# A block-sparse attention with a channel mix: every engine's order planned anew, with other transfer constants

## The chip, the cores and the metric

The kernel runs on one core of a Trainium2 chip. The metric is the device time of one execution in microseconds (us); less is better. The core has five engines with an instruction stream of its own each: PE (matrix products; its weight loads, PEld, run beside them), DVE, ACT and POOL (element-wise work), and SP, which here issues the transfers from and to HBM. An engine works its stream strictly in order, and waits where an instruction needs what another engine or a transfer hasn't finished.

## The reference

Attention over 24 blocks of 32 positions (4 batches, 8 heads, 768 positions, head size 64). A block of queries sees its own block and both neighbours, blocks 0 and 23, and three sampled blocks; the queries of blocks 0 and 23 see everything. A channel mix follows, in which a token is blended with the one before it.

```python
scores = scale * np.matmul(q, k.transpose(0, 1, 3, 2))
mask = np.abs(blk_i - blk_j) <= window
mask = mask | (blk_i == 0) | (blk_j == 0) | (blk_i == n_blocks - 1) | (blk_j == n_blocks - 1)
for qb in range(n_blocks):
    for kb in sampled_blocks[qb]:
        mask[qb * block:(qb + 1) * block, kb * block:(kb + 1) * block] = True
scores = np.where(mask, scores, -1000000000.0)
attn = np.exp(scores - np.max(scores, axis=-1, keepdims=True))
attn = attn / (np.sum(attn, axis=-1, keepdims=True) + 1e-09)
x = np.matmul(attn, v)            # heads joined: (4, 768, 512)
xk = mu_k * x + (1.0 - mu_k) * x_prev
xr = mu_r * x + (1.0 - mu_r) * x_prev
k = np.maximum(xk @ w_k, 0.0)     # (512, 1024)
v = k * k @ w_v                   # (1024, 512)
r = 1.0 / (1.0 + np.exp(-(xr @ w_r)))
return r * v
```

## The kernel before

**Attention** is cut into 26 units. Four wide units (numbers 0 to 3, in the order 0, 1, 3, 2 here) hold the queries of blocks 0 and 23 of one batch each and all 768 keys. Twenty-two near units (4 to 25) hold one block of queries each, for all batches, and eight blocks of keys. A unit goes through these steps, in two halves: PE makes the scores `s` (`sw` in a wide unit; L608, L559); DVE takes their maxima `nm` (L613 to L618, L567); ACT the exponentials `p` (L539); PE transposes them into `t` (L523), ACT copies these into `pt` (L527); PE multiplies by the values `VA` into `o` (L639, L585); DVE divides into `x` (L657 to L661), PE transposes it (L668), ACT puts it into the mixer's tile `xt`. There are two PSUM buffers each for scores, for `o`, and for transposes (the latter shared with the mixer).

**The sampled blocks** are numbers in HBM. Two small transfers bring them and a table of constants (`number` and `con`, L307 and L308), 17 rows on DVE (L316 to L336, "the pack") drop those that the mask holds already and write them into `packed`; SP reads `packed` (L425) and issues the transfers of the sampled keys (L488) and values (L505) of every near unit.

**The mixer** has 12 tiles of 256 tokens. A tile has two gates `r_0p`, `r_1p` (12 matmuls each, L776), four hidden parts `h_0p` to `h_3p` (24 each, L794) whose squares ACT and POOL make in the buffers tagged "kk" (L807 to L811), and two products with w_v (L823). A product is made of three terms in a rounded format, for which each operand is split in a high and a low part.

**The weights** come as 64-bit numbers in 20 chunks (0 to 3 of w_r, 4 to 11 of w_k, 12 to 19 of w_v; 512 KB each) and are converted on the chip: ACT makes `wmag` (L373), also in a "kk" buffer, of which there are three; DVE makes `wf` of it in three steps (L378, L382, L386); POOL splits that (L396, L400). The first twelve are loaded into eight slots (`early_w`), the last eight (`raw`) into buffers that they share with the exponentials `p`.

**The order** is not written out. The code declares operations with their cost, their reads and writes and a rank (a due time), and `Plan.order` goes through a model of the five engines: at each step it takes, for each engine, the operation of lowest rank among those that could start within `NEAR` ns of the first, and emits the one that ends first. A transfer takes its bytes over `RATE` (bytes per ns) in that model, on one queue, and is noticed `DONE` ns later; eight may be under way (`FLIGHT`). Buffers are given out in the same pass. So the constants of the model and the table of due times at the end of the file fix the order of all engines and which operation gets which buffer. The ranks are sums such as these:

```python
plan.add(DVE, 4000, PICK + 3, pack, reads=[(number,), (con,)], writes=[(r,), (e,), (packed,)])
at = RAW_AT[i] if i < 3 * CC else rank
at_k, at_v = at - LEAD_K, at - LEAD_V
plan.add(PE, N_PV, t1 + O_PV[kind], pv, ...)
```

`UNIT_AT` holds the due times of the units, `MIX_AT` of the mixer tiles, `RAW_AT` of the early weight loads, `WEIGHT_AT` of the conversions, `PICK` of the pack and its two transfers, `LEAD_*` how long before a unit its loads are due, `O_*` the distances of a unit's steps.

## Time and profile before

| | us |
|---|---|
| three runs | 571.64, 572.94, 573.92 (median 572.94) |
| the profiled execution | 571.98 |
| its span, from the first to the last instruction | 570.2 |
| PE busy | 537.7 |
| DVE, ACT, POOL busy | 269.6, 325.2, 291.0 |
| mean granted PE clock | 0.987 |

The span is cut off at the first and last instruction; 1.78 us of the execution lie around it. In rows of a timeline the first number is the start, the second the busy time of the row, then engine, line, operation and tiles (buffer numbers left out), and in brackets how long the engine was idle ahead of it and what ended that. Releasers are worked out from semaphore events: where an instruction waits for several, the one named can be one that was long done.

### The profile page before, as it was taken

The numbers are of one execution on the slowest core, as the hardware profiler recorded it, in microseconds if no ns is written. First come the engines' busy times: TensorE is split into PE (matmuls) and PEld (weight loads), VectorE is DVE, ScalarE is ACT, GpSimd is POOL, SyncE is SP. The second block draws the span as 40 slices with busy tenths as digits, with TensorE's granted clock in tenths as the row PEclk, the third lists the DMA queues.
The fourth block names the chain that finished last, engine by engine and source line by source line (L and its number), as shares of the span: only waits on it lengthen the run. The fifth ranks groups of instructions, "written<-read, shape, count | busy, mean of one in ns | idle before, by whom it ended". The sixth has DMA issues, their size and how long they took to land.

```text
span 570.2 us, 18311 instructions
## 1 busy us (share of the span) xinstructions
PE 537.7 (94%) x7724; PEld 438.5 (77%) x7724; DVE 269.6 (47%) x533; ACT 325.2 (57%) x612; POOL 291.0 (51%) x359
## 2 busy tenths in 40 slices
PE   6788778979999999999999999999999999999997
PEld 2454556856887798897798798887877989889886
DVE  0877998887445353434424524433452242142411
ACT  0676687768478468467464756546564356424330
POOL 0430456887266066346066285373383663448752
PEclk9799899999999999999999999999999999999999
DMA  8999899773653553362651804135510302110001
GB/s 314 395 398 342 295 343 352 260 228 94 192 182 95 172 164 116 112 189 76 189 167 29 278 24 157 36 100 166 169 39 20 95 19 84 32 39 1 20 20 38
DMA packets 34183, 86.09 MB, mean 151 GB/s; under 512 B 5010, under 2 KB 5780, under 8 KB 31124
## 3 DMA queue, kind: packets, MB, share of 16 engines
q1 hardware_dynamic: 34100, 84.92, 44.5%
q8 instruction: 61, 1.00, 0.7%
q14 instruction: 22, 0.18, 0.1%
HBM read 78.60 MB, written 6.29 MB: 149 GB/s over the span
## 4 chain that ended last, share of the span: by engine, by line
PE 80%; DVE 9%; DMA 4%; ACT 2%; POOL 2%; issue 2%; SPq 0%; DVEq 0%; ACTq 0%
PE v L823 23%; PE o L585 6%; PE s L559 6%; PE t L523 6%; PE r_0p L776 5%; PE h_1p L794 5%; PE h_3p L794 5%; PE h_0p L794 5%; PE h_2p L794 5%; PE r_1p L776 4%; PE tw L523 2%; PE sw L608 2%; DVE nm L567 2%; PE tx L668 2%; DMA raw<-w_v 1%
## 5 line engine op out<-in xcount | busy, mean ns | idle before, releaser
L823 PE MATMUL v<-wv,k 128*128 128x512 f32 (+1 forms) x600 | 145.0, 391 | 0.0
L823 PEld LDWEIGHTS v<-wv,k 128*128 128x128 f32 x600 | 106.8, 188 | 22.8 <-DVE x L661 0.8
L539 ACT ACTIVATE p<-s,nm 128x256 f32<-128x256 f32 x176 | 104.1, 728 | 18.1 <-DVE nm L569 13.8
L567 DVE TENSOR_REDUCE nm<-s 128x4 f32<-128x1024 f32 x44 | 53.6, 1219 | 16.1 <-PE s L559 16.1
L523 PE MATMUL t<-ident,p 128*128 128x128 f32 x352 | 54.6, 278 | 4.7 <-ACT z L783 2.4
L585 PE MATMUL o<-VA,pt 128*32 128x65 f32 x2816 | 49.9, 222 | 6.7 <-ACT pt L527 4.0
L585 PEld LDWEIGHTS o<-VA,pt 128*32 128x32 f32 x2816 | 42.3, 109 | 16.9 <-issue 9.7
L752 POOL TENSOR_TENSOR xr<-xr_1f,xr 128x256 fp32r<-128x256 f32 x24 | 17.7, 737 | 70.8 <-ACT xr L750 70.8
L523 PEld LDWEIGHTS t<-ident,p 128*128 128x128 f32 x352 | 40.2, 140 | 16.1 <-ACT z L783 2.9
L527 ACT COPY pt<-t 128x512 f32<-128x512 f32 x68 | 40.7, 604 | 18.7 <-PE t L523 15.7
L559 PE MATMUL s<-KA,q 64*32 64x256 f32 x1408 | 46.5, 387 | 1.6 <-DVE wf L386 1.2
L743 DVE SCALAR_TENSOR_TENSOR xr_1f<-xr_1d,mk,xt 128x128 f32<-128x128 f32 x48 | 17.9, 372 | 55.9 <-POOL xr L752 46.3
L831 DVE SCALAR_TENSOR_TENSOR z<-v,z 128x512 f32<-128x512 f32 (+1 forms) x25 | 16.8, 670 | 50.1 <-PE v L823 50.0
L685 ACT COPY xt<-tx 128x512 f32<-128x512 f32 x22 | 13.0, 591 | 42.1 <-PE tx L668 42.0
L794 PE MATMUL h_0p<-xk,wk 128*128 128x256 f32 x288 | 37.0, 282 | 0.0
L776 PE MATMUL r_1p<-wr,xr 128*128 128x512 f32 x144 | 36.4, 400 | 0.6 <-ACT h_3k L807 0.6
L794 PE MATMUL h_3p<-xk,wk 128*128 128x256 f32 x288 | 36.4, 281 | 0.0
L743 DVE SCALAR_TENSOR_TENSOR xr_0f<-xr_0d,mk,xt 128x128 f32<-128x128 f32 x48 | 20.3, 424 | 34.0 <-POOL xk L752 13.9
L776 PE MATMUL r_0p<-wr,xr 128*128 128x512 f32 x144 | 36.4, 400 | 0.0
L794 PE MATMUL h_1p<-xk,wk 128*128 128x256 f32 x288 | 36.3, 281 | 0.0
L794 PE MATMUL h_2p<-xk,wk 128*128 128x256 f32 x288 | 36.3, 280 | 0.0
L794 PEld LDWEIGHTS h_0p<-xk,wk 128*128 128x128 f32 x288 | 35.1, 188 | 0.7
(139 smaller groups left out, 940.1 us busy)
## 6 DMA issues: line engine op xcount, KB each, us to landing
VA<-vt SPq DMA_DIRECT2D x93, 260.0 KB, 3.8
KA<-kt SPq DMA_DIRECT2D x90, 256.0 KB, 3.7
VA<-vw SPq DMA_DIRECT2D x24, 260.0 KB, 6.1
KA<-kq SPq DMA_DIRECT2D x16, 384.0 KB, 6.7
out<-z SPq DMA_DIRECT2D x23, 256.0 KB, 2.2
q<-qt SPq DMA_DIRECT2D x22, 256.0 KB, 4.3
early_w<-w_k SPq DMA_DIRECT2D x8, 512.0 KB, 6.4
raw<-w_v SPq DMA_DIRECT2D x8, 512.0 KB, 5.0
```

The source lines that it names most:

```text
L523: nc.tensor.transpose(tp.ap[:, i, :], p.ap[:, x : x + P], ident.ap)
L527: plan.add(ACT, 200 + 0.75 * P * many, rank + 0.1, lambda: nc.scalar.copy(pt.ap[:, 0:many], tp.ap[:, 0:many]), reads=[(tp,)], writes=[(pt,)])
L539: plan.add(ACT, 262 + 0.83 * width, rank, lambda: nc.scalar.activation(turned(p.ap[:, out]), view(), AF.Exp, bias=nm(), scale=SCALE), read ...
L559: nc.tensor.matmul(s.ap[ROWS[j], row, a * 256 : (a + 1) * 256].rearrange("p (n x) -> p n x", x=BLK), q.ap[half, (hp * QB + j) * BLK : (hp ...
L567: nc.vector.tensor_reduce(out=nm.ap.rearrange("p (r a) -> p r a", r=2), in_=s.ap.rearrange("p r (a x) -> p r a x", a=2), axis=AX.X, op=ALU ...
L585: nc.tensor.matmul(o[gi].ap[ROWS[j], i * DV : (i + 1) * DV], pts[row].ap[:, 2 * a + g, ROWS[j]], VA.ap[:, c0 + g, j, h * DV : (h + 1) * DV ...
L743: nc.vector.scalar_tensor_tensor(out=parts(f.ap[:, i, :]), in0=parts(d.ap), scalar=mk.ap[:, which, c : c + 1], in1=cols(c, 1), op0=ALU.mul ...
L752: plan.add(POOL, 80 + 2.4 * MIX * tw, rank + O_MIX, lambda f=f, cs=cs: nc.gpsimd.tensor_tensor(out=dst.ap[:, 1, cs], in0=f.ap, in1=dst.ap[ ...
L776: nc.tensor.matmul(pr.ap[:, 0:512], xr.ap[:, a, c, :], wr.ap[:, w, c, :], start=(c == 0 and m == 0), stop=(c == CC - 1 and m == 2))
L794: nc.tensor.matmul(ph.ap[:, ff * TT : (ff + 1) * TT], wk.ap[:, w, c, f * P : (f + 1) * P], xk.ap[:, a, c, :], start=(c == 0 and m == 0), s ...
L823: nc.tensor.matmul(pv.ap[:, 0:width], k2.ap[:, a, f, i * P : (i + 1) * P], wv.ap[:, w, f, cs], start=(f == 0 and m == 0), stop=(f == FC - ...
L831: plan.add(DVE, 150 + 1.05 * width, done, lambda pv=pv, cs=cs: nc.vector.scalar_tensor_tensor(out=z.ap[:, cs], in0=pv.ap[:, 0:width], scal ...
```

## The change

Two constants of the model of transfers, the due time of the pack, and the table of due times and distances are replaced. No operation is added, removed or altered, and the code of the planner stays as it is; the order that it gives is another on every engine. In the diff, of the table, two lines are shown:

```diff
-    RING, RING_POOL, RATE, DONE, DONE_POOL = 650, 1000, 370, 670, 2600
+    RING, RING_POOL, RATE, DONE, DONE_POOL = 650, 1000, 335, 900, 2600
...
-PICK = -10.949
+PICK = 5.0
...
-LEAD_W, LEAD_Q, LEAD_K, LEAD_V = 31.394, 58.736, 95.899, 26.261
+LEAD_W, LEAD_Q, LEAD_K, LEAD_V = 30.562, 60.235, 742.902, 12.723
-NEAR, STAY, STORE = 34.076, -1.502, 639.005
+NEAR, STAY, STORE = 55.741, 2.392, 639.005
...
```

**The loads of the pack.** On SP, in the wide units' loads, before (four weight loads, the loads of unit 0 and the query of unit 1 stand ahead of these rows; names carry the number of their buffer):

```order
L364 DMA early_w_98<-w_r 128x1024
L471 DMA VA_68<-vw 128x520 x6
L467 DMA KA_67<-kq 128x768 x4
L471 DMA VA_68<-vw 128x520 x4
L461 DMA q3_187<-qt 128x256
L471 DMA VA_68<-vw 128x520 x2
L307 DMA number_262<-blocks 1x144
L308 DMA con_272<-seen 1x462
L364 DMA early_w_98<-w_k 128x1024 x2
L467 DMA KA_67<-kq 128x768 x4
```

and of the change (five weight loads, the loads of unit 0 and the query of unit 1 stand ahead):

```order
L364 DMA early_w_98<-w_k 128x1024
L471 DMA VA_68<-vw 128x520 x6
L364 DMA early_w_98<-w_k 128x1024
L467 DMA KA_67<-kq 128x768 x4
L364 DMA early_w_98<-w_k 128x1024 x2
L461 DMA q3_197<-qt 128x256
L471 DMA VA_68<-vw 128x520 x6
L307 DMA number_375<-blocks 1x144
L308 DMA con_386<-seen 1x462
L467 DMA KA_67<-kq 128x768 x2
```

Before, five weight loads (L364) precede `number` and `con`, and four keys' loads of unit 3 stand behind two further ones. Now nine weight loads precede them, and unit 3's first keys come straight after.

On DVE, where the pack begins, before (`nmw3_0` are maxima of unit 3, the second half that is worked):

```order
L617 TENSOR_TENSOR nmw2_1_616<-nmw2_1_616 128x2
L618 TENSOR_SCALAR nmw2_1_616<-nmw2_1_616 128x2
L613 TENSOR_REDUCE nmw3_0_672<-sw3_0_0_656 128x2
L613 TENSOR_REDUCE nmw3_0_672<-sw3_0_1_674 128x2
L617 TENSOR_TENSOR nmw3_0_672<-nmw3_0_672 128x2
L618 TENSOR_SCALAR nmw3_0_672<-nmw3_0_672 128x2
L316 CAST pickf_691<-number_262 1x72
L318 TENSOR_TENSOR equal_692<-pickf_691,con_272 1x22x7 x2
L320 TENSOR_TENSOR equal_692<-pickf_691 1x22
```

and of the change (`wf8` and `wmag9` are conversions of weight chunks 8 and 9, `nmw1_0` maxima of unit 1):

```order
L613 TENSOR_REDUCE nmw1_0_394<-sw1_0_1_400 128x2
L382 SCALAR_TENSOR_TENSOR wmag8_392<-early_w_98,wmag8_392 128x512
L617 TENSOR_TENSOR nmw1_0_394<-nmw1_0_394 128x2
L618 TENSOR_SCALAR nmw1_0_394<-nmw1_0_394 128x2
L386 SCALAR_TENSOR_TENSOR wf8_440<-early_w_98,wmag8_392 128x512
L378 TENSOR_SCALAR wmag9_405<-wmag9_405 128x512
L316 CAST pickf_475<-number_375 1x72
L318 TENSOR_TENSOR equal_476<-pickf_475,con_386 1x22x7 x2
L320 TENSOR_TENSOR equal_476<-pickf_475 1x22
```

Where it ends now (`nmw3_1` is the first half of unit 3 that is worked):

```order
L334 CAST pickf_475<-pickf_475 1x48
L335 TENSOR_SCALAR packed_69<-pickf_475 1x24
L336 TENSOR_TENSOR packed_69<-packed_69,pickf_475 1x24
L613 TENSOR_REDUCE nmw3_1_548<-sw3_1_0_510 128x2
L613 TENSOR_REDUCE nmw3_1_548<-sw3_1_1_543 128x2
L382 SCALAR_TENSOR_TENSOR wmag9_405<-early_w_98,wmag9_405 128x512
L617 TENSOR_TENSOR nmw3_1_548<-nmw3_1_548 128x2
L618 TENSOR_SCALAR nmw3_1_548<-nmw3_1_548 128x2
L386 SCALAR_TENSOR_TENSOR wf9_619<-early_w_98,wmag9_405 128x512
```

Before, the pack follows the last maxima of unit 3 and precedes those of `nmw2_0`. Now it stands two halves earlier, between a conversion and the first maxima of unit 3. Seven conversions have begun ahead of it (5, 10, 1, 4, 0, 8 and one step of 9), against six before (0, 5, 1, 8, 4, 10).

**The values of unit 6.** On PE, in the first mixer tile, before (`h0_0p` is the first hidden part, `o6_1` and `t6_0_0` belong to unit 6):

```order
L559 MATMUL s7_0_1610<-KA_67,q7_1337 32x256 x16
L668 MATMUL tx5_1633<-ident_66,x5_1495 128x128 x4
L794 MATMUL h0_0p_1657<-xk0_1540,wk_71 128x256 x12
L585 MATMUL o6_1_1678<-VA_68,pt6_1_0_1497 32x65 x16
L585 MATMUL o6_1_1678<-VA_68,pt6_1_1_1566 32x65 x16
L523 MATMUL t6_0_0_1720<-ident_66,p6_0_1568 128x128 x4
L794 MATMUL h0_0p_1657<-xk0_1540,wk_71 128x256 x12
L523 MATMUL t6_0_1_1747<-ident_66,p6_0_1568 128x128 x4
```

and of the change:

```order
L559 MATMUL s7_0_1610<-KA_67,q7_1304 32x256 x16
L668 MATMUL tx5_1633<-ident_66,x5_1497 128x128 x4
L794 MATMUL h0_0p_1657<-xk0_1547,wk_71 128x256 x12
L523 MATMUL t6_0_0_1678<-ident_66,p6_0_1565 128x128 x4
L794 MATMUL h0_0p_1657<-xk0_1547,wk_71 128x256 x12
L585 MATMUL o6_1_1707<-VA_68,pt6_1_0_1495 32x65 x16
L585 MATMUL o6_1_1707<-VA_68,pt6_1_1_1563 32x65 x16
L523 MATMUL t6_0_1_1748<-ident_66,p6_0_1565 128x128 x4
```

`o6_1` has moved behind the transpose `t6_0_0` and the second twelve matmuls of `h0_0p`.

**The copy of unit 7.** On ACT, later in that tile, before (`wmag13` and `wmag18` are conversions of w_v, `h0_2k` and `k20` the two steps of a hidden part, `pt7_0_1` the copy of a transpose of unit 7):

```order
L373 ACTIVATE wmag18_1927<-raw18_1783 128x512
L527 COPY pt7_0_0_1942<-t7_0_0_1917 128x512
L807 ACTIVATE h0_2k_1980<-h0_2p_1895 128x512
L808 ACTIVATE k20_1790<-h0_2k_1980 128x512
L373 ACTIVATE wmag13_2000<-raw13_1841 128x512
L527 COPY pt7_0_1_2021<-t7_0_1_1986 128x512
L685 COPY xt1_1407<-tx6_1995 128x4x4x32
L688 COPY xt2_2062<-tx6_1995 128x4x4
```

and of the change:

```order
L373 ACTIVATE wmag13_1912<-raw13_1777 128x512
L539 ACTIVATE p7_0_1887<-s7_0_1610,nm7_0_1654 128x2x4x32
L527 COPY pt7_0_0_1934<-t7_0_0_1915 128x512
L539 ACTIVATE p7_0_1887<-s7_0_1610,nm7_0_1654 128x2x4x32
L373 ACTIVATE wmag12_1940<-raw12_1817 128x512
L807 ACTIVATE h0_2k_1986<-h0_2p_1890 128x512
L527 COPY pt7_0_1_2008<-t7_0_1_1978 128x512
L808 ACTIVATE k20_1746<-h0_2k_1986 128x512
```

Ahead of `pt7_0_1` stands now the conversion of chunk 12 in place of that of chunk 13; the step `k20` of the hidden part, which stood ahead of it, stands behind it, and one exponential of unit 7 has come between the two copies.

More of the change, by code (lines that the diff above doesn't have):

```diff
@@ L899 @@
 LAST = 10
[L901 to L911 removed]
+O_MAX, O_EXP, O_TR = [-159.93, 341.66, -2392.61, -181.95], [16.15, 433.56, -434.19, 224.65], [11.95, -1.93, 20.62, -269.57]
+O_PV, O_END = [-686.48, 14.64, -922.61, -243.09], [22.94, 16.16, 22.86, -393.74]
+SECOND = [-4.21, 4.56, -12.32, -3.38]
+LEAD_W, LEAD_Q, LEAD_K, LEAD_V = 30.562, 60.235, 742.902, 12.723
+O_MIX, O_SQ, O_SQ_FIRST = -19.876, 79.118, 4.369
+NEAR, STAY, STORE = 55.741, 2.392, 639.005
+UNIT_AT = [-21.26, 6.72, 42.39, 39.16, 56.42, 62.70, 75.38, 83.64, 102.13, 110.71, 127.62, 134.14, 149.24, 160.18, 223.52, 234.38, 242.78, 265.39, 312.30, 324.78, 332.52, 370.58, 384.19, 392.94, 409.49, 472.96]
+MIX_AT = [83.64, 121.35, 149.72, 206.75, 239.30, 295.89, 323.08, 371.32, 400.75, 443.73, 587.11, 1170.17]
+MIX_RATE, MIX_RATE_LAST = 1.383, 22.313
+RAW_AT = [-54.01, -1920.79, 55.44, 34.09, -31.96, -489.62, 41.69, -862.82, -8.12, -23.29, -36.97, -522.56]
+WEIGHT_AT = [-363.02, -530.14, 41.46, 75.20, -419.35, -805.17, 9.28, 24.77, -240.82, -220.17, -783.29, 66.22, 98.06, 97.22, 86.73, 101.25, 94.97, 88.88, 104.57, 89.00]
 def kernel(**inputs):
```

9 lines of the change are left out of this document (removed).

## The prediction

> **What bounds the kernel now.** I read the page first, for the busy shares; then busy time by stretches of 20 us, for where PE idles; then PE's timeline, for what each idle ended on; last the timelines of ACT, DVE and SP at those places.
>
> ```profile
> span 570.2 us, 18311 instructions
> PE 537.7 (94%) x7724; PEld 438.5 (77%) x7724; DVE 269.6 (47%) x533; ACT 325.2 (57%) x612; POOL 291.0 (51%) x359
> L523 PE MATMUL t<-ident,p 128*128 128x128 f32 x352 | 54.6, 278 | 4.7 <-ACT z L783 2.4
> 0.00:20.00 20.00, 12.90 (x52) 4.52 (x56) 5.47 (x9) 5.34 (x9) 2.67 (x9) 0.81 0.92 337
> 20.00:40.00 20.00, 17.88 (x390) 11.41 (x382) 16.79 (x29) 13.55 (x29) 8.15 (x8) 0.93 1.04 397
> 40.00:60.00 20.00, 15.97 (x407) 10.15 (x406) 15.59 (x45) 13.86 (x30) 2.16 (x4) 1.00 0.97 348
> 60.00:80.00 20.00, 15.50 (x408) 10.10 (x412) 19.69 (x29) 14.30 (x32) 11.13 (x11) 0.91 0.92 315
> 80.00:100.00 20.00, 16.69 (x425) 12.26 (x417) 16.75 (x37) 15.26 (x31) 13.12 (x18) 1.00 0.95 343
> 100.00:120.00 20.00, 16.23 (x349) 13.69 (x342) 15.75 (x27) 12.53 (x24) 18.15 (x19) 1.00 0.72 241
> 120.00:140.00 20.00, 18.12 (x246) 14.39 (x236) 17.44 (x26) 18.24 (x35) 15.81 (x16) 1.00 0.55 170
> 140.00:571.00 431.00, 424.42 (x5499) 362.01 (x5497) 162.09 (x337) 232.10 (x428) 219.82 (x278) 1.00 0.32 100
> 566.90 0.42 DVE L831 SCALAR_TENSOR_TENSOR z<-v,z 128x256 f32<-128x256 f32 x1 [2.35 <-PE v L823]
> ```
>
> The columns of the stretches are length, busy time of PE, PEld, DVE, ACT and POOL, granted clock, DMA share, GB/s. PE works 537.7 of 570.2 us and is idle for 32.5. After 140 us it works 424.4 of the 430.2 that are left: 5.8 idle, of which 3.3 (570.2 − 566.9) is the tail behind the last matmul and some 2.4 a wait on a gate's copy. So 26.7 us of the idle lie before 140, and no order can save more than these and the 5.8. There transfers (share 0.92 to 1.04 up to 100 us), DVE (19.69 of 20 us from 60 to 80) and POOL (18.15 from 100) are in turn nearly full. These are the waits the change touches:
>
> ```profile
> 16.96 1.56 PE L608 MATMUL sw<-KA,q 64*64 64x384 f32 x8 [3.09 <-ACT pw L539]
> 60.94 1.15 PE L639 MATMUL o<-VA,ptw 128*32 128x65 f32 x64 [2.24 <-ACT ptw L527]
> 63.25 1.24 PE L559 MATMUL s<-KA,q 64*32 64x256 f32 x24 [1.17 <-DVE wf L386]
> 99.16 1.04 PE L585 MATMUL o<-VA,pt 128*32 128x65 f32 x57 [1.60 <-DMA VA<-vt]
> 119.75 0.67 PE L585 MATMUL o<-VA,pt 128*32 128x65 f32 x32 [3.39 <-ACT pt L527]
> ```
>
> **The change, part by part.** It adds and removes no work; the sum of instructions per engine is what it was, so every term is a wait won or lost.
>
> **A, the first exponentials.** ACT's first conversion is now that of the fourth load, not of the w_r chunk for which it waited here:
>
> ```profile
> 15.31 0.66 ACT L373 ACTIVATE wmag<-early_w 128x512 f32<-128x512 f32 x1 [13.28 <-DMA early_w<-w_r]
> ```
>
> The first exponential can come up to 0.66 us earlier. But the fourth now stands behind two conversions of 0.66, so the score buffer that it frees comes up to 1.3 later. I take 0, with −0.7 and +1.3 as ends; part B's wait lies behind it.
>
> **B, the pack of the sampled blocks.** DVE works these 17 rows between unit 3's and unit 2's reductions now; afterwards they stand before unit 3's first, behind the conversion of weight chunk 8.
>
> ```profile
> 36.27 0.90 DVE L386 SCALAR_TENSOR_TENSOR wf<-early_w,wmag 128x512 int32<-128x512 int32 x1
> 39.26 1.26 DVE L378 TENSOR_SCALAR wmag<-wmag 128x512 int32<-128x512 int32 x1
> 40.63 0.17 DVE L618 TENSOR_SCALAR nmw<-nmw 128x2 f32<-128x2 f32 x1
> 51.07 0.18 DVE L316 CAST pickf<-number 1x72 f32<-1x72 int32 x1
> 55.86 0.18 DVE L336 TENSOR_TENSOR packed<-packed,pickf 1x24 int32<-1x24 int32 x1
> 55.97 1.80 DVE L613 TENSOR_REDUCE nmw<-sw 128x2 f32<-128x768 f32 x2
> 57.14 2.35 SPq L488 DMA_DIRECT2D KA<-kt x3
> 40.84 2.00 ACT L539 ACTIVATE pw<-sw,nmw 128x384 f32<-128x384 f32 x4
> 43.23 0.65 PE L523 MATMUL tw<-ident,pw 128*128 128x128 f32 x4
> ```
>
> The pack lasts 51.07 to 56.04, 4.97 us. Afterwards it starts at about 36.0, as one conversion of the two that end at 37.17 here comes later: 36.0 + 4.97 = 41.0. Then come unit 3's two reductions (1.8), one step of a conversion (0.69) and the small ones (0.33): unit 3's maxima are ready at 43.8 instead of 40.8, 3.0 later. The transpose at 43.23 has only some 0.9 us of slack (it needs three of four exponentials that take 2.00 from 40.84, to 42.35): **a new PE wait of 2.1 us**. What goes in return: the pack no longer stands before unit 2's reductions (55.97), and three conversions no longer stand ahead of unit 2's copies on ACT, so the 2.24 at 60.94 goes. The 1.17 at 63.25, put down to a conversion that was done, is rather the sampled keys, which SP issues only after the pack: they can go some 8 us earlier. B = +2.1 − 2.24 − 1.17 = **−1.3**. Ends: −3.4 (the new wait is filled by other PE work), and +5.9 (the rival of the late pack, below).
>
> The new wait needs the pack's two small loads on time, and SP issues them behind more bytes: before them stand nine 512-KB weight loads instead of five.
>
> ```profile
> 23.28 0.31 SPq L307 DMA_DIRECT2D number<-blocks  x1
> 23.97 0.22 SPq L308 DMA_DIRECT2D con<-seen  x1
> early_w<-w_k SPq DMA_DIRECT2D x8, 512.0 KB, 6.4
> DMA to landing us min/median/max: 4.0/5.9/8.5
> ```
>
> Four loads more are 2048 KB, 2.10 MB; at the 397 GB/s of the stretch from 20 to 40 that is 5.3 us. The second small load goes out at 23.97 + 5.3 = 29.3. Its landing isn't shown; the nearest rows, the key loads from 20 to 60, have 4.0 to 8.5, median 5.9 (the weight loads 6.4): 33.3 to 37.8, at the median 35.2, against the 36.0 at which the pack wants it. I take it as just in time. The Trainium skill ("DMA: Bandwidth & Descriptors", the note on three numbers under the bandwidth derivation) puts the HBM limit per core at about 358 GB/s; by that the four loads would take an estimated 5.9 us, but this trace moved 397 for 20 us on end, so the measurement stands.
>
> **C, the values of unit 6.** Afterwards one transpose and the second twelve of h_0's matmuls stand ahead of the o of unit 6 that waits 1.60 for its values.
>
> ```profile
> 95.94 1.62 PE L794 MATMUL h_0p<-xk,wk 128*128 128x256 f32 x12
> 91.85 2.21 ACT L539 ACTIVATE p<-s,nm 128x256 f32<-128x256 f32 x4
> ```
>
> Twelve take about 1.6 us and the transpose 0.6, together more than the wait, and the transpose's exponentials are done at 94.06. **−1.6**; ends −1.6 and 0 (if the transfer, not PE, sets what follows).
>
> **D, the copy of unit 7.** The 3.39 at 119.75 comes about because ACT works in order: the copy stands behind a conversion whose buffer POOL had to free.
>
> ```profile
> 111.93 0.70 ACT L373 ACTIVATE wmag<-raw 128x512 f32<-128x512 f32 x1 [1.80 <-DVE wf L386]
> 113.44 0.60 ACT L807 ACTIVATE h_2k<-h_2p 128x512 f32<-128x512 f32 x1 [0.34 <-POOL k L811]
> 118.55 0.67 ACT L373 ACTIVATE wmag<-raw 128x512 f32<-128x512 f32 x1 [3.85 <-POOL k L811]
> ```
>
> Afterwards the conversion ahead of the copy uses a buffer that DVE frees, and h_2's first step stands there too, which waits for POOL. So the waits of the first two rows move ahead of the copy: 3.39 − 1.80 − 0.34 = 1.25 won. **−1.2**; ends −3.4 (nothing new) and +1.5 (a wait of 3.85, and h_2's 0.60 and 0.34, in place of 3.39, rounded up).
>
> **E, after 140.** Shorter lists between a unit's scores and their use, and another end. PE is busy 424.4 of 430.2 and the other engines half: **0**; ends −2.5 (all idle but the tail) and +1.2 (one new wait as long as the one at 63.25).
>
> Sum: 0 − 1.3 − 1.6 − 1.2 + 0 = −4.1. The profiled execution took 571.98, its span 570.2 and 1.78 around it: 567.9. It lies 0.96 under the median of the runs shown, 572.94; on that footing the forecast is **568.8**.
>
> **The rivals.**
>
> *More flows through.* The pack moves from the stretch where DVE is full (19.69 of 20) to one where it has 3.2 us free (16.79). If no new PE wait comes and D goes whole: −3.4 − 1.6 − 3.4 = −8.4, so 564.5. Against it: five waits of the same stretch must all go and none come.
>
> *Transfers bind.* The DMA share is 0.92 to 1.04 to 100 us, and the order moves no byte out of that time. Then what B and C win is spent waiting for the next load, and D alone stays: −1.2, so 571.7. For it speaks the share; against it that only two of the five waits above were followed to a load.
>
> *The pack comes late, and the kernel is slower.* DVE works in order: if the second small load lands after 36.0, unit 3's reductions behind the pack wait for it, ACT's exponentials for them, PE for those. At the row's longest landing, 8.5, or the longest weight load's 9.1, it is there at 37.8 to 38.4: 2.4 more, PE's wait 4.5. Longer than the 3.39 that left the clock whole, it would also cost clock:
>
> ```profile
> 15.00:20.00 5.00, 3.04 (x16) 1.32 (x20) 3.47 (x7) 4.05 (x8) 1.90 (x2) 0.50 1.05 397
> 60.00:65.00 5.00, 2.90 (x97) 1.86 (x98) 5.00 (x6) 2.69 (x5) 4.23 (x4) 0.86 0.85 272
> 65.00:70.00 5.00, 4.79 (x120) 3.24 (x124) 4.90 (x9) 3.03 (x6) 2.38 (x3) 0.79 0.91 298
> 115.00:120.00 5.00, 1.61 (x80) 0.97 (x68) 2.58 (x5) 1.45 (x3) 5.00 (x5) 1.00 0.57 179
> ```
>
> At 60 to 70 it lost 0.14 × 2.90 + 0.21 × 4.79 = 1.4 us. With the conversions pushed back too, the waits at 60.94 and 63.25 stay: 4.5 + 1.4 − 1.6 = +4.3, so 577.2. It is slower by over 0.5% from a landing at about 37.3 on (2.1 + 1.3 + 1.4 − 1.6 = +3.2). For it: the 2.10 MB; against it: the median, 35.2.
>
> *The clock alone.* The pack is on time, but the new wait of 2.1 falls with others into one stretch and the clock drops there: +1.4 on the forecast, 570.2. The rows are divided: 0.50 at 15 to 20 after waits of 3 us, 1.00 at 115 to 120 with 3.39 idle at once. The Trainium skill ("TensorE: Matmul & The Clock Gate", Part 1) has the clock fall to half after an idle window of about 3.4 us, with windows that run freely; by that rule 2.1 us alone would seldom do it, and the trace agrees as far as 3.39 did not.
>
> **How the numbers follow.** Forecast 0.36, more flows through 0.14, transfers bind 0.26, the late pack 0.18, the clock alone 0.06. The range reaches from 564.5 to 576.5: it takes in all cases but half of the best and half of the worst, about 0.16. A measurement can tell 0.5%, 2.9 us, so faster is under 570.1 and slower above 575.8. Faster: 0.29 of the forecast's 0.36 and the 0.14, 0.43. Slower: 0.16 of the late pack's 0.18. The rest, 0.41, is the same.
>
> **What would show it.** B: the pack on DVE near 36 to 41, a PE wait of about 2 us on exponentials near 43, none of over 1 us at 60 to 64, keys for unit 4 issued before 50. If the pack starts after 37, the late pack is right. C: no wait on values near 99. D: a wait before unit 7's o of about 2 us near 117. E: 5 to 6 us idle after 140; if the idle there has grown by 3 us or more, my reading of the later order was wrong, and with it the sign. If B to D show as said and the stretch to 140 is no shorter, transfers bind.

## The result, and the profile after

The changed kernel takes 579.73 us (median of 4 runs, 577.60 to 581.29), the kernel before, beside it on the same chip, 572.51. The ratio is 1.0121, with a 95% interval of 1.0078 to 1.0164: **slower by 1.2%**, some 7 us. The forecast was 568.8 with a range to 576.5, so sign and range were both wrong.

The page of the changed kernel, its span and the busy time of each engine:

```profile
span 577.0 us, 18299 instructions
PE 539.1 (93%) x7724; PEld 439.8 (76%) x7724; DVE 270.4 (47%) x533; ACT 327.4 (57%) x612; POOL 291.3 (50%) x359
```

Against before (span 570.2, PE 537.7) PE works 1.4 us more and idles 5.4 more: 37.9 against 32.5. The stretches of the changed kernel, in the columns of the prediction (length, PE, PEld, DVE, ACT, POOL, clock, DMA share, GB/s), show where:

```profile
0.00:20.00 20.00, 11.05 (x45) 3.74 (x46) 4.49 (x8) 4.66 (x8) 2.65 (x9) 0.80 0.91 337
20.00:40.00 20.00, 16.22 (x350) 10.22 (x354) 19.17 (x33) 14.53 (x30) 10.20 (x10) 0.95 0.92 338
40.00:60.00 20.00, 14.53 (x314) 8.66 (x302) 12.21 (x35) 9.01 (x21) 1.88 (x2) 0.91 0.93 316
60.00:80.00 20.00, 13.59 (x428) 9.95 (x426) 16.77 (x28) 14.21 (x30) 7.90 (x8) 1.00 0.92 302
80.00:100.00 20.00, 18.14 (x462) 12.81 (x451) 13.36 (x33) 16.60 (x36) 10.26 (x14) 1.00 0.95 333
100.00:120.00 20.00, 18.36 (x363) 15.64 (x366) 18.48 (x30) 14.16 (x27) 17.70 (x18) 1.00 0.81 308
120.00:140.00 20.00, 16.64 (x287) 13.17 (x286) 18.48 (x26) 16.58 (x29) 18.85 (x18) 0.91 0.59 194
140.00:180.00 40.00, 39.00 (x634) 32.82 (x635) 17.81 (x43) 23.12 (x48) 16.75 (x23) 0.96 0.47 146
180.00:577.00 397.00, 391.58 (x4894) 332.79 (x4893) 149.69 (x302) 214.57 (x389) 205.11 (x261) 1.00 0.30 95
```

Subtracting the PE column from the length, stretch by stretch, and comparing with before: up to 80 us PE is idle 24.6 instead of 17.8, from 80 to 120 only 3.5 instead of 7.1, from 120 to 140 again 3.4 instead of 1.9. So the order loses 6.9 us early, gets 3.6 of it back where C and D were expected, and loses again at the end of the first mixer tile. PE's 1.4 us more of work go with the clock: it is 0.91 at 40 to 60 and at 120 to 140 and 0.96 at 140 to 180, where before had 1.00; from 60 to 80 it is the other way round (1.00, before 0.91).

These are the waits of PE in the changed kernel that answer to the ones of before (start, busy time, engine, line, operation, and in brackets the idle time ahead and what ended it):

```profile
48.10 0.88 PE L608 MATMUL sw<-KA,q 64*64 64x384 f32 x8 [3.54 <-ACT pw L539]
66.17 0.66 PE L523 MATMUL tw<-ident,pw 128*128 128x128 f32 x4 [1.62 <-ACT ptw L527]
76.25 1.14 PE L639 MATMUL o<-VA,ptw 128*32 128x65 f32 x64 [1.64 <-ACT ptw L527]
123.38 0.67 PE L585 MATMUL o<-VA,pt 128*32 128x65 f32 x32 [1.73 <-ACT pt L527]
141.00 0.66 PE L668 MATMUL tx<-ident,x 128*128 128x128 f32 x4 [2.63 <-DVE pt L529]
```

B's new wait is there and longer than forecast (3.54, not 2.1). The 2.24 and the 1.17 that it should have bought are replaced by 1.62 and 1.64. C's wait on values is gone; D's fell from 3.39 to 1.73, near the 2.1 that were forecast. And 2.63 at 141.00 is new: a wait that no term of the sum held.

**The end of the first tile (E).** DVE of the changed kernel ahead of 141.00, and in the last row POOL:

```profile
135.94 1.75 DVE L386 SCALAR_TENSOR_TENSOR wf<-raw,wmag 128x512 int32<-128x512 int32 x1 [1.18 <-POOL wv L400]
137.62 1.21 DVE L567 TENSOR_REDUCE nm<-s 128x4 f32<-128x1024 f32 x1
138.94 1.40 DVE L743 SCALAR_TENSOR_TENSOR xr_0f<-xr_0d,mk,xt 128x128 f32<-128x128 f32 x1
140.26 0.68 DVE L529 COPY pt<-t 128x512 f32<-128x512 f32 x1
138.93 1.27 POOL L400 TENSOR_TENSOR wv<-wf,wv 128x512 fp32r<-128x512 f32 x1
```

PE waits for the copy at 140.26, the last of unit 8. Ahead of it on DVE stand a maximum of unit 9 and a blend of the next gate, for which PE does not wait here, and the blend takes 1.40 us instead of some 0.34 (its length at 136.51 in the kernel before), from POOL's start at 138.93 to just after POOL's end at 140.20. The same three rows stand in the same order in the kernel before, with a blend as long. These are PE's matmuls ahead of the wait, the wait, and DVE's blend and copy in the kernel before, and last the matmuls ahead of the wait in the changed kernel:

```profile
132.33 2.34 PE L823 MATMUL v<-wv,k 128*128 128x512 f32 x9
135.91 0.66 PE L523 MATMUL t<-ident,p 128*128 128x128 f32 x4 [1.24 <-DVE pt L529]
133.82 1.43 DVE L743 SCALAR_TENSOR_TENSOR xr_0f<-xr_0d,mk,xt 128x128 f32<-128x128 f32 x1
135.18 0.68 DVE L529 COPY pt<-t 128x512 f32<-128x512 f32 x1
136.72 1.65 PE L823 MATMUL v<-wv,k 128*128 128x512 f32 x6
```

The wait grew by 1.39 us, from 1.24 to 2.63, in two halves: PE has six matmuls of v ahead of it instead of nine (0.69 us less), and the copy starts 0.7 us later, counted from the start of these matmuls. It is no chance of one execution: the three other traces of kernels that keep these rows (after_again, q0_ahead and pack_back, below) show it too, and longer:

```profile
140.54 1.12 PE L668 MATMUL tx<-ident,x 128*128 128x128 f32 x4 [3.43 <-DVE pt L529]
142.26 0.66 PE L668 MATMUL tx<-ident,x 128*128 128x128 f32 x4 [3.43 <-DVE pt L529]
138.87 1.12 PE L668 MATMUL tx<-ident,x 128*128 128x128 f32 x4 [3.23 <-DVE pt L529]
```

Behind it the clock falls in all four. The changed kernel's stretches of 5 us behind D's wait and around this one:

```profile
125.00:130.00 5.00, 5.00 (x51) 4.71 (x58) 4.93 (x8) 4.32 (x9) 4.77 (x5) 0.71 1.01 355
140.00:145.00 5.00, 4.00 (x13) 3.24 (x14) 2.36 (x7) 2.11 (x6) 2.52 (x5) 0.66 0.32 98
```

That is another 0.29 × 5.00 = 1.5 us in the first, and in the second, where PE is busy in all the time at the lower clock, 0.34 × 5.00 = 1.7. Behind D's wait the fall is not the rule: in q0_ahead and pack_back the same wait is 1.70 and 1.73, and the clock stays at 1.00.

**The pack (B).** DVE of the changed kernel at the first rows of the pack, at its last, and at the maxima behind it, and in the last two rows POOL at that time:

```profile
37.89 0.60 DVE L316 CAST pickf<-number 1x72 f32<-1x72 int32 x1
38.52 1.61 DVE L318 TENSOR_TENSOR equal<-pickf,con 1x154 f32<-1x154 f32 x2
44.18 0.18 DVE L336 TENSOR_TENSOR packed<-packed,pickf 1x24 int32<-1x24 int32 x1
46.79 0.17 DVE L618 TENSOR_SCALAR nmw<-nmw 128x2 f32<-128x2 f32 x1
37.70 0.74 POOL L396 CAST wk<-wf 128x512 fp32r<-128x512 f32 x1 [2.69 <-DVE wf L386]
38.52 1.45 POOL L400 TENSOR_TENSOR wk<-wf,wk 128x512 fp32r<-128x512 f32 x1
```

The pack began at 37.89, not at 36.0, and lasted 6.47 us (to 44.36), not 4.97. The 1.5 are in its first two rows: 0.60 instead of 0.18, and the second of the L318, which starts at 38.76, took 1.38 instead of 0.30. They end 0.1 and 0.2 us behind the POOL rows beside them (38.44 and 39.97). Unit 3's maxima were ready at 46.96 instead of 40.80: forecast 3.0 later, measured 6.2.

The Trainium skill ("SBUF — State Buffer", section "SBUF: two separate sides") says that DVE and GpSimd, which is POOL here, share a pair of ports under an exclusive lock: a DVE operation with two inputs in SBUF blocks for the whole of a GpSimd operation that reads SBUF, if that one began first. The rows agree: the second L318 and the blend start behind POOL's operation and end with it, however small they are (to 0.2 and 0.1 us), and where POOL is idle the L318 are short (pack_back, below); no run moved POOL's rows alone.

SP of the changed kernel, the pack's two loads and later a key load and the sampled keys (L488):

```profile
29.60 0.31 SPq L307 DMA_DIRECT2D number<-blocks  x1
29.95 0.22 SPq L308 DMA_DIRECT2D con<-seen  x1
56.63 0.33 SPq L443 DMA_DIRECT2D KA<-kt  x1
58.11 1.79 SPq L488 DMA_DIRECT2D KA<-kt  x3
```

and from the view of SP's waits in its first 100 us (total, times, longest):

```profile
SPq L443 <- PE sw L608: 5.7, 3, 5.1
```

The second small load went out at 29.95, 0.7 us later than forecast, but DVE's rows ahead of the pack show no wait for it: other rows, conversions and maxima, kept DVE busy up to 37.89. So "the late pack" (577.2) came near the result by luck: its sign is there (a start after 37), its cause, late loads, is not. And the sampled keys, ready to go from 44.4, went at 58.11, a microsecond later than before (57.14). Ahead of them in SP's order stands a key load that waits 5.1 us for a buffer that PE still reads.

### The profile page after: what moved, and what is told of

It reads as the page before. It is cut to its first block, busy times and chain, and to the rows that moved or that the text cites. A ratio compares the mean times of both kernels' runs of the same rounds, so it can differ in the third digit from the quotient of the medians.

```text
span 577.0 us, 18299 instructions
## 1 busy us (share of the span) xinstructions
PE 539.1 (93%) x7724; PEld 439.8 (76%) x7724; DVE 270.4 (47%) x533; ACT 327.4 (57%) x612; POOL 291.3 (50%) x359
## 4 chain that ended last, share of the span: by engine, by line
PE 71%; DVE 14%; ACT 6%; DMA 3%; POOL 2%; issue 2%; SPq 1%; DVEq 0%; ACTq 0%; POOLq 0%
PE v L823 21%; PE o L585 6%; PE r_0p L776 5%; PE h_0p L794 5%; PE t L523 5%; PE h_2p L794 5%; PE h_1p L794 5%; PE h_3p L794 5%; PE s L559 5%; PE r_1p L776 3%; DVE nm L567 2%; DVE wf L386 2%; DVE wmag L382 2%; PE sw L608 2%; ACT p L539 2%
## 5 line engine op out<-in xcount | busy, mean ns | idle before, releaser
L823 PE MATMUL v<-wv,k 128*128 128x512 f32 (+1 forms) x600 | 147.1, 394 | 0.8 <-ACT z L783 0.8
L539 ACT ACTIVATE p<-s,nm 128x256 f32<-128x256 f32 x176 | 105.7, 736 | 29.8 <-DVE nm L569 27.7
L527 ACT COPY pt<-t 128x512 f32<-128x512 f32 x68 | 41.1, 609 | 27.8 <-PE t L523 27.5
L743 DVE SCALAR_TENSOR_TENSOR xr_1f<-xr_1d,mk,xt 128x128 f32<-128x128 f32 x48 | 17.9, 372 | 53.8 <-POOL xr L752 44.0
L743 DVE SCALAR_TENSOR_TENSOR xr_0f<-xr_0d,mk,xt 128x128 f32<-128x128 f32 x48 | 19.7, 411 | 40.0 <-POOL xr L752 17.4
L794 PE MATMUL h_3p<-xk,wk 128*128 128x256 f32 x288 | 38.3, 287 | 0.0
L740 POOL TENSOR_TENSOR xr_1d<-xt 128x128 f32<-128x128 f32 x48 | 21.2, 441 | 29.7 <-DVE xr_1f L743 21.3
```

The source lines that it names most:

```text
L527: plan.add(ACT, 200 + 0.75 * P * many, rank + 0.1, lambda: nc.scalar.copy(pt.ap[:, 0:many], tp.ap[:, 0:many]), reads=[(tp,)], writes=[(pt,)])
L539: plan.add(ACT, 262 + 0.83 * width, rank, lambda: nc.scalar.activation(turned(p.ap[:, out]), view(), AF.Exp, bias=nm(), scale=SCALE), read ...
L740: sub.tensor_tensor(out=parts(d.ap), in0=cols(c, 0), in1=cols(c, 1), op=ALU.subtract)
L743: nc.vector.scalar_tensor_tensor(out=parts(f.ap[:, i, :]), in0=parts(d.ap), scalar=mk.ap[:, which, c : c + 1], in1=cols(c, 1), op0=ALU.mul ...
L794: nc.tensor.matmul(ph.ap[:, ff * TT : (ff + 1) * TT], wk.ap[:, w, c, f * P : (f + 1) * P], xk.ap[:, a, c, :], start=(c == 0 and m == 0), s ...
L823: nc.tensor.matmul(pv.ap[:, 0:width], k2.ap[:, a, f, i * P : (i + 1) * P], wv.ap[:, w, f, cs], start=(f == 0 and m == 0), stop=(f == FC - ...
```

## The experiments

All take the planner's finished list and move single operations behind others, so that one piece of the order is put back (or brought into the kernel before) with all else as it was:

```diff
-    for op in plan.order():
+    for op in moved(plan):
...
+def moved(plan):
+    ops = plan.order()
+    for which, other in BEHIND:
+        ops.remove(plan.named[which])
+        ops.insert(ops.index(plan.named[other]) + 1, plan.named[which])
+    return ops
```

Below stands only each kernel's list, with the order that it starts from. In the names, `q0` is the query load of unit 0, `kq2_1_0` a key load of wide unit 2, `kt4_0` the three key loads of unit 4 and `keys1` its sampled keys; `nmw3_0` and `nm9_1` are maxima of units 3 and 9, `pt8_1_1` and `ptw3_0_0` copies (L527, L529) of units 8 and 3, `xr1_0m2` is a blend (L743), `ow2_1_0` a product of unit 2, `sign1`, `wf4`, `hi4` and the like steps of the conversion of chunks 1 and 4, `mag13` the first of chunk 13. Where not said otherwise, each ran 6 to 12 times beside the kernel before; ratios are to that kernel's runs.

### The three suspects of the changed order, one at a time and together

All start from the changed kernel. q0_ahead puts the query of unit 0 ahead of its first keys again:

```diff
+BEHIND = [('kq0_1_0', 'q0'), ('kq0_1_1', 'kq0_1_0')]
```

pack_back puts the pack behind the last maxima of unit 3:

```diff
+BEHIND = [('pack', 'nmw3_0'), ('keys1', 'pack')]
```

pt8_ahead puts the copy of unit 8 ahead of the blend and the maximum:

```diff
+BEHIND = [('xr1_0m2', 'pt8_1_1'), ('nm9_1', 'pt8_1_1')]
```

three_back holds all three lists.

> The changed kernel with one edit: the query of unit 0 is loaded ahead of unit 0's first two key loads, as before, not behind them. In the changed kernel PE's first scores start at 12.93 us, after a wait of 5.55 for that query; before they started at 10.81. Theory (what the start loses is carried to the end, since the chain from scores over maxima and exponentials to the next unit is tight from there on): first scores near 10.8, every later place some 2 us earlier, span 577.0 - 2.1 = 574.9. Rival (the stretch to 80 us is bound by transfers and conversions, so the start costs nothing): the first scores come 2 us earlier, the lag is gone again by 60 us, span 576.5 to 577.5. Second rival (the late query is chance and not the order): first scores stay near 12.9.

> The changed kernel with one edit: on DVE the 17 rows of the pack stand behind unit 3's last maxima, as before, not ahead of its first. Theory (the pack's place costs): the wait of 3.54 us of PE at 48 us goes, and the clock loss of 1.2 us at 40 to 60 with it; the pack then holds unit 2's last maxima for about 1.8 us, as before. Net -1.8 to -3.0, span 574 to 575. Rival (the pack had to be paid somewhere in this chain): the wait only moves to 55 to 65 us, span 576.5 to 577.5. A sign of contention: the pack's first rows take 0.60 and 1.38 us in the changed kernel, beside two POOL instructions, where they took 0.18 and 0.30 before; away from them they should be short again.

> The changed kernel with one edit: on DVE the copy of unit 8's last transpose stands ahead of unit 9's second maxima and of a blend for the mixer, not behind them. It does not begin then before 137.6, instead of 140.26. Theory (the late loss comes from this one place where DVE's order holds PE, and from the clock that drops behind it): PE's wait of 2.63 us at 141 shrinks to under 0.5, the clock of 0.66 at 140 to 145 is 1.00, which is worth another 1.4; span 577.0 - 2.5 - 1.4 = 573.1, perhaps 0.7 less won as the maxima come later. Rival (the mixer's first product waits there for its squares and weights whatever the copy does): another wait at 138 to 146 takes its place, span 576 to 577.

> The changed kernel with the three edits at once (unit 0's query ahead, the pack behind unit 3's maxima, unit 8's copy ahead). Theory (three separate losses that add up): -2.1 - 2.4 - 3.5 = -8.0, span 569, about the time of the kernel before or some 2 us under it, since the two waits at 99 and 119 us that the change removed stay removed. Rival (the losses are one chain, and a later limit of transfers or conversions takes back what the start wins): span 573 or more.

| kernel | median us | ratio to before | 95% |
|---|---|---|---|
| after | 579.73 | 1.0121 | 1.0078 to 1.0164 |
| q0_ahead | 579.80 | 1.0127 | 1.0090 to 1.0163 |
| pack_back | 578.32 | 1.0094 | 1.0069 to 1.0120 |
| pt8_ahead | 576.75 | 1.0056 | 1.0030 to 1.0081 |
| three_back | 575.06 | 1.0052 | 1.0027 to 1.0077 |

The query at the start carries nothing: the first scores came at 10.93 instead of 12.93, but the first gate came no earlier (97.85, in the change 95.50). The copy of unit 8 carries 0.65 points, about half of the whole loss (3.7 us by the ratios, 3.0 by the medians). Its interval does not meet that of q0_ahead and overlaps that of the change by a hair. In its trace the wait is 0.80 where it was 2.63, and the rows behind are at clock 1.00:

```profile
140.65 0.66 PE L668 MATMUL tx<-ident,x 128*128 128x128 f32 x4 [0.80 <-DVE pt L529]
```

The mean granted clock of the runs rose with it, from 0.9795 to 0.9856. From the first gate of tile 0 to that of tile 1 the four traces without this edit (the change twice, q0_ahead, pack_back) take 62.8 to 64.3 us, the two with it (pt8_ahead, three_back) 60.4 and 60.6, and the kernel before 61.0. So in these traces this place is the whole loss behind the first gate; the rest lies ahead of that gate.

The pack put back alone gives 0.27 points, and the intervals overlap, though the long rows went as the theory said; POOL is idle where the pack stands now, and the rows are short again (L318 in pack_back: minimum, median and maximum in ns):

```profile
L318 DVE TENSOR_TENSOR equal<-pickf,con x3: 300/301/307, 52.0 to 52.6; 1x154 f32<-1x154 f32 x3
```

PE of pack_back says where the gain went:

```profile
62.50 1.04 PE L523 MATMUL tw<-ident,pw 128*128 128x128 f32 x4 [4.15 <-ACT ptw L527]
```

The wait of 3.54 at 48 became one of 4.15 at 62.50. ACT's order was planned for the early pack and has the exponentials of unit 2 ahead of the copies of unit 3, so with the pack back PE waits for those copies. All three together leave 0.52%, which can't be told from the 0.56% of the copy alone; the span near 569 that was expected did not come.

### What is left

Each of these kernels adds entries to a list. four_back adds to three_back, so that ACT's copies of unit 3 come earlier:

```diff
+    ('ptw3_0_0', 'ow2_1_0'), ('ptw3_0_1', 'ow2_1_1'),
```

five_back adds to four_back, so that steps of two conversions come later on DVE and POOL:

```diff
+    ('sign1', 'nmw0_0'), ('shift4', 'nmw1_1'), ('sign4', 'shift4'),
+    ('wf4', 'sign4'), ('hi4', 'wf4'), ('lo4', 'hi4'),
```

six_back adds to four_back, so that on SP the query and three key loads of unit 4 go ahead of its sampled keys:

```diff
+    ('keys1', 'kt4_0'),
```

six_q adds to six_back, so that four key loads of the wide units go ahead of the query of unit 2:

```diff
+    ('q2', 'kq2_0_1'), ('kq3_0_0', 'q2'), ('kq3_0_1', 'kq3_0_0'),
```

> The kernel with three edits (unit 0's query ahead, the pack behind unit 3's maxima, unit 8's copy ahead) and a fourth: on ACT the copies of unit 3's first two transposes stand ahead of most exponentials of unit 2 and of two weight conversions, nearly as before. With the three edits alone PE waited 4.16 us at 63.67 for such a copy, since ACT worked the exponentials of unit 2 first, and those wait for the pack. Theory (the pack's place and ACT's order belong together: each was planned for the other): the wait falls to about 2, and the unit's last values come some 2 us earlier; span 571.9 - 1.5 = 570.4. Rival (from 60 to 130 us conversions on DVE and POOL set the pace, so this wait costs nothing at the end): the wait goes, the mixer's first product still starts at 134, span 571.5 to 572.5.

> The four edits and a fifth: on DVE five conversion steps (one of weight chunk 1, all of chunk 4) stand behind the maxima of units 0 and 1 that they held up, with POOL's split of chunk 4 behind them. They take 0.7 to 1.6 us each there. Theory (with the first three edits the scores of unit 1 still come 0.8 to 1.5 us later than before, because of these): scores of unit 1's second half at 29.8 instead of 31.15, everything behind as much earlier up to 60 us, and at the end 1.0 won against four edits: span 569.5. Rival (conversions have to be done by 90 us in any case): nothing won at the end, span as with four edits.

> The kernel with four edits (unit 0's query ahead, the pack behind unit 3's maxima, unit 8's copy ahead, two of ACT's copies ahead) and one on SP: the query and three key loads of unit 4 stand ahead of the loads of the sampled keys, as before, not behind them. With four edits SP issues nothing between 50.1 and 56.8 us, since the sampled keys' loads wait for the pack, and PE then waits 4.29 us until 67.44 for unit 4's scores, whose query was issued at 58.7. Theory (what is left of the loss, 0.5%, is SP's order around the pack, on which the near units hang): SP's gap holds only the sampled keys, unit 4's scores come at 64.5 or before, the mixer's first product 2 us earlier, span 571.1 - 2.5 = 568.6, ratio 0.998 to 1.002. Rival (from there to 130 us conversions set the pace): scores earlier, first product still at 134, span 570.5 to 571.5, ratio 1.004 or more.

> The four edits and the one on SP, and one more on SP: four key loads of the wide units stand ahead of the query of unit 2, which waits for PE, as before the change. Theory that the queue runs dry: all kernels with the new order moved 277 to 358 GB/s between 30 and 40 us, those with the old order 397 to 400, since those keys need nothing and stand behind a query whose buffer PE still reads; now 380 or more there, the first gate (r0) by 91.5 instead of 92.1 to 96.6, and a ratio of 0.999 to 1.002. Rival, that the loss comes from the conversions and the clock between 40 and 80: the queue may be fuller, but r0 stays beyond 92 and the ratio at 1.003 to 1.006.

| kernel | median us | ratio to before | 95% | first score of unit 4 | first gate |
|---|---|---|---|---|---|
| four_back | 575.78 | 1.0051 | 1.0023 to 1.0079 | 67.4 | 93.4 |
| five_back | 576.04 | 1.0063 | 1.0041 to 1.0084 | 69.8 | 95.6 |
| six_back | 575.01 | 1.0046 | 1.0024 to 1.0067 | 64.1 | 92.1 |
| six_q | 573.85 | 1.0041 | 1.0017 to 1.0064 | 63.9 | 92.7 |

(The last two columns are starts in us on PE in the profiled execution; in that of before they are 63.25 and 90.66, in that of the change 69.30 and 95.50.) The copies of unit 3 and the two conversions carry nothing that can be measured. The SP edit did what it should: the score of unit 4 starts at 64.1 instead of 67.4, and the profiled execution of six_back had a span of 570.0, as before the change. Its twelve runs say otherwise, 0.46% slower. Single executions of the same kernel and of the changed one, profiled anew, show how far one profiled execution stands for its runs:

> The kernel with all five edits once more, for a second profile: its first profiled execution was its fastest of 12, 3 us under the median. If what is left of the loss is a wait that comes in most executions but not in that one, this profile shows it, with a span of 572 to 574: a wait of PE that the first did not have, of 1.5 us or more, between 10 and 140 us. If it is the clock, the mean clock is lower by 0.003 or more and the waits are alike. If the first was chance in timing alone, the span is near 570 again.

> The same kernel a third time, for the same question: the span between 570 and 574, with the difference to the first profile either in one wait of PE between 10 and 140 us or in the clock.

> The changed kernel once more, for a second profile. The first showed the first scores at 12.93 us after a wait of 5.55 for unit 0's query; in three runs of edits that leave that load where it is they came at 11.7 to 11.8. If the place of the load costs 1 us as a rule and 2 by chance, the first scores come at 11.7 to 11.8 here; the waits of 3.54 at 48 us and of 2.63 at 141 us are there again within 0.8.

They took 572.28, 575.73 and 578.24, with the first gate at 92.6 in the first and at 96.6 in the second: what the profiled six_back shows is one of its better executions, and nearly 4 us lie between two executions of one program. In after_again the first scores came at 11.63, and the waits of 3.54 and 2.63 were there again, with 3.82 and 3.43.

In the rows of 30 to 40 us one difference ran through all traces: the old order moves 397 to 400 GB/s there, the new one 277 to 358. With a query waiting for PE, four key loads that wait for nothing stand behind it on SP. six_q puts these back; before_q2 gives the kernel before this piece of the new order:

```diff
+BEHIND = [('kq2_1_0', 'q2'), ('kq2_1_1', 'kq2_1_0'), ('kq2_0_0', 'kq3_0_1'), ('kq2_0_1', 'kq2_0_0')]
```

> The kernel before with one edit on SP: the query of unit 2 ahead of four key loads of the wide units, as the change has it. Theory that the queue runs dry: below 360 GB/s between 30 and 40 us, the first gate 1 us or more later than 90.7, ratio 1.003 to 1.006. Rival, that a short gap in the queue is made up before the keys are used: ratio 0.999 to 1.002.

The stretch from 30 to 40 us of six_back:

```profile
30.00:40.00 10.00, 8.21 (x168) 4.50 (x157) 7.24 (x16) 7.54 (x17) 3.91 (x4) 1.00 0.91 319
```

of six_q:

```profile
30.00:40.00 10.00, 8.22 (x161) 4.51 (x150) 7.24 (x15) 7.53 (x17) 3.91 (x4) 1.00 1.02 368
```

and of before_q2:

```profile
30.00:40.00 10.00, 8.65 (x188) 5.60 (x181) 9.02 (x16) 7.29 (x17) 4.46 (x4) 1.00 0.92 331
```

In six_q the queue is full again (share 1.02, though 368 GB/s is short of the 380 expected), yet PE's busy time does not change, the ratio stays at 1.0041, and before_q2 with 331 GB/s took 572.82, ratio 1.0014 with an interval (0.9998 to 1.0031) that holds no change. Its first gate did come late in the profiled execution, at 92.43, as the theory had it; that execution (574.54) was the slowest of its twelve. By the ratios the rival holds in both: the gap in the queue is real and costs little (0.3% at most) or nothing.

### The parts of the change, alone in the kernel before

All start from the kernel before. before_c does C alone:

```diff
+BEHIND = [('t6_0_0', 'h0_0mm0'), ('h0_0mm1', 't6_0_0')]
```

before_d does D: conversion 13 goes behind the copy of unit 7:

```diff
+BEHIND = [('mag13', 'pt7_0_1')]
```

before_q0 puts the query of unit 0 behind its first keys, as the change does:

```diff
+BEHIND = [('q0', 'kq0_1_1')]
```

before_pt8 puts the copy of unit 8 ahead, as pt8_ahead does:

```diff
+BEHIND = [('xr1_0m2', 'pt8_1_1'), ('nm9_1', 'pt8_1_1')]
```

before_cd holds the lists of before_c and before_d, before_pt8_d those of before_pt8 and before_d.

> The kernel before with one edit, the change's own at the place called C: a transpose of unit 6 and the second twelve matmuls of the first hidden part stand ahead of unit 6's first product with the values. Theory (C was rightly sized): the wait of 1.60 us at 99 us goes, and the end comes 1.6 earlier, span 568.6. Rival (what is won is given back, because conversions on DVE and POOL set the pace to 140 us): a later wait grows by as much, span 569.8 to 570.6.

> The kernel before with one edit at the place called D: ACT's conversion of weight chunk 13 stands behind the copy of unit 7's transpose, not ahead of it. Theory (the wait of 3.39 us at 119.75 is ACT's order alone): the wait goes but for 0.4 us, span 570.2 - 3.0 = 567.2. Rival (POOL, which is full from 105 to 135 us and frees the conversion's buffer, sets the pace): the weights of the last product are ready no earlier, the mixer's first product or unit 8's copy waits instead, span 569.5 to 570.5.

> The kernel before with both edits, C and D. Theory: both waits go and the sum of both is won at the end, span 570.2 - 4.6 = 565.6. Rival (pace of POOL and DVE up to 140 us): one at most is won, span 568.5 or more.

> The kernel before with one edit, the change's own at the start: the query of unit 0 is loaded behind unit 0's first two key loads. Theory (the place of that load costs some 2 us, and they are carried to the end): first scores near 12.9 instead of 10.81, span 572.2. Rival (it costs at the start, but the stretch to 80 us takes it back): first scores near 12.9, span 570 to 570.8. Second rival (the late query was not the order's doing but that of the weight load issued next): first scores stay near 10.8 to 11.5.

> The kernel before with one edit: the same as was made in the changed kernel, on DVE the copy of unit 8's last transpose ahead of unit 9's second maxima and of a blend. PE waits 1.24 us for it at 135.91 before. Theory (behind some 135 us PE has no other waits, so one that goes there is won whole at the end, while waits that go earlier are given back): wait under 0.3, the first gate of the second mixer tile 1.0 to 1.2 us earlier, span 569.1. Rival (given back here too): span 570 to 570.5.

> The kernel before with that edit and with D (ACT's conversion of chunk 13 behind unit 7's copy), the two that have a chance to win anything. Theory: 1.1 of the copy and about 1.0 of D, which alone measured 0.9987 of before: span 568.1, ratio 0.996 to 0.9975. Rival (both lie in the same chain of POOL and DVE to the first product, so only one counts): span 569 to 569.5, ratio 0.998 or more.

| kernel | median us | ratio to before | 95% | first matmul of v | first gate of tile 1 |
|---|---|---|---|---|---|
| before, profiled | 571.98 | | | 132.33 | 151.66 |
| before_c | 572.41 | 1.0013 | 0.9992 to 1.0034 | 132.75 | 151.09 |
| before_d | 571.69 | 0.9987 | 0.9970 to 1.0005 | 130.94 | 150.33 |
| before_cd | 572.19 | 1.0003 | 0.9986 to 1.0019 | 131.36 | 150.79 |
| before_q0 | 572.21 | 1.0006 | 0.9985 to 1.0026 | 132.55 | 151.12 |
| before_pt8 | 571.83 | 0.9989 | 0.9969 to 1.0008 | 132.45 | 150.38 |
| before_pt8_d | 570.36 | **0.9965** | 0.9949 to 0.9982 | 131.17 | 149.19 |

C, expected to bring 1.6 us, brings nothing: its interval leaves out the 0.28% that this would be. In the trace of before_c the wait on values is gone and v starts no earlier, though the first gate, which lies ahead of the edit, came at 88.11 instead of 90.66. Here the clock took it. These are the wait for unit 7's copy, as long as before, and the rows around and behind it:

```profile
118.07 1.10 PE L585 MATMUL o<-VA,pt 128*32 128x65 f32 x32 [3.39 <-ACT pt L527]
115.00:120.00 5.00, 1.93 (x36) 1.75 (x37) 2.68 (x3) 3.13 (x7) 5.00 (x6) 0.75 0.81 280
120.00:125.00 5.00, 5.00 (x28) 5.00 (x28) 4.93 (x10) 2.96 (x6) 3.89 (x3) 0.57 0.88 280
```

The second row alone is 0.43 × 5.00 = 2.2 us. So this trace does not show where C's microseconds would have gone. D takes its wait away, and PE of before_d gives most of it back within 9 us:

```profile
116.21 0.55 PE L585 MATMUL o<-VA,pt 128*32 128x65 f32 x23 [1.01 <-issue]
119.21 0.44 PE L523 MATMUL t<-ident,p 128*128 128x128 f32 x2 [0.86 <-ACT p L539]
120.27 0.44 PE L523 MATMUL t<-ident,p 128*128 128x128 f32 x2 [0.62 <-ACT p L539]
124.58 0.73 PE L776 MATMUL r_1p<-wr,xr 128*128 128x512 f32 x2 [0.99 <-ACT h_3k L807]
```

These four are 3.48 together, against the 3.39 of the wait that went; 0.64 of the last stood there before, so 2.84 are new. In before_cd, whose clock is at 1.00 from 95 to 160, both waits are gone, 4.99 us, and v starts 0.97 earlier, 0.25 of which the first gate had already (90.41). At the copy of unit 8, PE of before_pt8 shows no wait ahead of the transpose:

```profile
134.64 0.60 PE L523 MATMUL t<-ident,p 128*128 128x128 f32 x4
```

The edit takes away the wait of 1.24 there and brings the gate of tile 1 forward by 1.28 in the profiled execution, but its runs alone can't be told from no change. With D it gives the fastest kernel of all, 0.35% under the kernel before, 2.0 us, with an interval clear of 1, as expected.

## Why the prediction was wrong

**The bound and where to look** were right: from tile 1's first gate to the end of the span before and before_pt8_d take 418.5 and 418.7 us and the changed kernel 417.6, so all is decided before 160 us.

**A** (0) held: the query's place changed nothing in either order (1.0127 against 1.0121, and 1.0006).

**B** (−1.3) failed, in three of its steps. *"36.0 + 4.97"*: 37.89 + 6.47, since the duration was carried over from a place where POOL is idle to one where it is not; the wait was 3.54, not 2.1. *"They can go some 8 us earlier"*: they went 1 us later, for only DVE's side of the move was read and not what stands ahead of the sampled keys on SP. And the waits at 60.94 and 63.25 were each replaced. By the sum, B is 3.54 + 1.62 + 1.64 − 2.24 − 1.17 = +3.4 in place of −1.3. What that costs at the end is smaller: with the pack back, 0.27 points, unclear; with the SP edit on top, about as little (1.0051 to 1.0046). The price of the late pack, 577.2, leaves out D's −1.2; with it that sum is 576.0.

**C and D** (−1.6 and −1.2) were right in the trace and wrong in their worth: both waits went as described, and alone in the kernel before they measure +0.13% and −0.13%, together +0.03%, each not to be told from nothing. D's −1.2 by itself lies inside its interval, but the −2.8 of both (0.49%) is far outside theirs. Of the idle time that D removes most comes back a few microseconds later, in waits on ACT and one for which the profile names nothing (before_d). This is the mechanism of "transfers bind" with another cause: what is won early is spent waiting. For C alone it is not shown.

**E** (0) is the step that is shown to have cost most. Its bound was "one new wait as long as the one at 63.25", +1.2; the wait that came was 2.63 (up to 3.43 in other executions), with a stretch at clock 0.66 behind it. By pt8_ahead it carries 0.65 of the 1.21 points, 3.7 us. The order was read to 120 us and beyond that only as busy shares ("PE is busy 424.4 of 430.2 and the other engines half"), so that the stretch from 120 to 140 stood in no term; yet the row that would have told was there: DVE's copy behind a blend beside POOL, a wait of 1.24 already in the kernel before ("some 2.4 a wait on a gate's copy" was the one that the prediction did look at). The prediction had set idle after 140 grown by 3 us as the mark of this error; the wait lies at 138.4 to 141.0, just ahead of that line, and idle after it grew only from 5.8 to 6.4. E alone did not turn the sign: with the copy ahead the kernel is still 0.56% slower than before.

**The sum.** Forecast and result are 10.9 us apart. E is 3.7 of it, the gains of C and D that did not come 2.8, the gain of B that did not come 1.3; the 3.1 that remain are about the loss ahead of the first gate (0.5%) that stays open below.

**The clock** was a rival with 0.06 and too small a place. The prediction tied it to waits longer than 3.39 us, or to several in one stretch, yet its own rows from 60 to 70 (0.86 and 0.79) stand behind waits of 2.24 and 1.17. Within kernels a run is the longer the lower its mean clock: one slope over the runs of all changed kernels gives some 250 us for a whole unit (167 runs), so that a step of 0.003 is 0.8 us. The changed kernel's runs stand at 0.9795, those of pt8_ahead at 0.9856: 1.5 of the 3.7 us go by that slope with the clock.

**Not settled** are the last 0.4 to 0.5%, some 2.5 us, that stay with five and six moves taken back. They arise ahead of the first gate, which starts at 92.1 to 96.6 against 88.1 to 90.8 in the kernels of the old order (92.4 in before_q2). Most of the new idle time lies from 60 to 70 us: there PE is idle 4.7 to 8.0 in the traces from three_back to six_q, 1.6 to 2.9 in all of the old order. These are that row before, in six_back, and the longest wait of PE in it:

```profile
60.00:70.00 10.00, 7.69 (x216) 5.10 (x220) 9.90 (x14) 5.71 (x11) 6.61 (x6) 0.83 0.88 285
60.00:70.00 10.00, 5.33 (x171) 3.90 (x170) 7.76 (x13) 5.95 (x14) 5.00 (x5) 0.98 0.89 275
68.69 0.41 PE L668 MATMUL tx<-ident,x 128*128 128x128 f32 x2 [2.62 <-DVE x L661]
```

That division stands on DVE among conversion steps, which had themselves waited 3.60 us for ACT up to 62.07; no run moved these. The start, the pack, SP's order ahead of unit 4 and the queue at 30 to 40 us are ruled out as its whole cause. The order of the weight conversions was tried for two chunks only; the nine weight loads that stand ahead of the pack's loads were not moved, since the conversions behind them follow their order.
